# Top-k attention and a gated feed-forward on one core: stages of a unit set one unit apart

## The chip, the cores and the metric

One core of a Trainium2 chip runs the whole kernel in one launch. The metric is the time of an execution in microseconds (us). The engines named below are PE (TensorE), DVE (VectorE), ACT (ScalarE), POOL (GpSimd) and SP, which issues nearly all transfers. Each takes its instructions strictly in the order in which the program issued them.

## The reference

For 8 batches with 8 heads of 576 tokens and 64 dimensions, attention keeps of each row of scores only what is at least the 32nd largest; its output, 4608 tokens by 512, goes through `(h * cos(h)) @ w_out` with `h = x @ w_in`:

```python
scores = scale * np.matmul(q, k.transpose(0, 1, 3, 2))
kth = np.partition(scores, -top_k, axis=-1)[..., -top_k:-top_k + 1]
scores = np.where(scores >= kth, scores, -1000000000.0)
attn = np.exp(scores - np.max(scores, axis=-1, keepdims=True))
attn = attn / (np.sum(attn, axis=-1, keepdims=True) + 1e-09)
x = np.matmul(attn, v)      # then (B,H,S,D) -> (B*S, H*D)
h = x @ w_in
return (h * np.cos(h)) @ w_out
```

q, k and v are float32. The weights arrive as 64-bit floats and are decoded to float32 on the chip, in 32 chunks of 128x512.

## The kernel before

**Units and slots.** A unit is 128 tokens of one pair of heads: 36 token tiles by 4 pairs, 144 units. The main loop (L523) runs one slot per unit, and each engine's queue is filled in the order written there. For a unit, `scores` (L192, PE) writes a 4-bank PSUM tile, of which there is one; `take_scores` (L207, ACT) copies it to one of three score buffers `s`, a slot ahead of the ranking. `topk_round` (L214, DVE) runs four times: the 8 largest of each row, then (three times) their replacement by a very low value, for both heads. `bounds` (L230) makes from the first and the 32nd value the two bounds, with two small POOL operations; `mask` and `exponentials` (ACT, L241 and L249) apply them in place and sum the rows into `den`; `reciprocal` (DVE, L258) adds 1e-9 and inverts; `normalise` (POOL, L264) scales. `split` (L274) separates the 16-bit halves on POOL and writes them to DRAM by SP; `transposes` (L283) reads them back transposed by a DMA; `values` (L308, PE) multiplies by v, and `take_values` (ACT) puts the result in `xT`.

**Which slot does what.** In slot i: ranking of unit i and scores of unit i+1; bounds, mask, exponentials, reciprocal, normalising and split of unit i-1, the reciprocal standing in DVE's queue between the second and the third part of the ranking of unit i; transposes of unit i-2; values of unit i-3. The first eight units don't go through DRAM: PE transposes them in the slot of their normalising (`transposes_now`, L291).

**Feed-forward.** It is fed between attention's matmuls in jobs: `ff1` (L356; four 128x128 by 256 products, 8 matmul instructions, into one of two banks `mm`) and `ff2` (L437; two products of 512 columns, 4 instructions, into the single bank `o2`; eight jobs make a row of 128 tokens). `feed` (L478) alternates the two kinds as far as inputs are there, at most two and then four a slot within a credit of four a slot, capped at five. `take_banks` (L386), called at the head of the slot and behind the first feeding, empties full banks on ACT; only the second call of a slot comes behind the exponentials. POOL reduces the angles (`reduce_first`, `reduce_second`), ACT takes the sine (`sines`), POOL multiplies (`gate`). A block is 256 tokens, eight units (the first four and the last two are 128), and needs one tile `g` per 1024 values; a new one is begun only while live tiles and staged weight chunks are fewer than `CHUNKS` (L93).

**Weights.** `load_weights` stages a chunk, `decode_first` (ACT, three operations), `decode_second` (DVE, two, L132 and L133) and `decode_third` (POOL, two) decode it; DVE's part runs from slot 1 on, POOL's part behind the slot's split.

Of the kernel before, what the change touches and what calls it, by code (L numbers as in the profile page):

```python
# [10 lines left out]
F32 = mybir.dt.float32  # L11
# [3 lines left out]
AF = mybir.ActivationFunctionType  # L15
ALU = mybir.AluOpType

P = 128
TOPK = 32
NEG = -3.4028234663852886e38  # L20
EPS = 1e-9
# [10 lines left out]
def kernel(  # L32
# [9 lines left out]
    nc = tc.nc  # L42
# [22 lines left out]
    make_identity(nc, ident)  # L65
    halfpi = consts.tile([P, 1], F32, tag="halfpi")
    nc.vector.memset(halfpi, math.pi / 2.0)

# [18 lines left out]
    for f in range(NF):  # L89
        w = consts.tile([P, DM], F32, tag=f"w_out{f}", name=f"w_out{f}")  # L90
        w_out.append(w)
        chunks.append((moe_w_out[f * P : (f + 1) * P, :], w))
    CHUNKS, XB = 9, 4  # L93
    ff = {"live": 0, "tick": 0, "now": 0, "credit": 0.0, "end": False, "kind": 0}

    wq = {"next": 0, "loaded": deque(), "second": deque(), "done": 0, "ready": 0}

    def load_weights(n):
        for _ in range(n):
            i = wq["next"]  # L100
            if i >= len(chunks):
                return
            src, dst = chunks[i]
            if not DECODE:
                nc.sync.dma_start(out=dst, in_=src)
                wq["next"] = wq["done"] = i + 1
                continue
            staging = len(wq["loaded"]) + len(wq["second"])
            if staging >= 6 or staging + ff["live"] >= CHUNKS:
                return  # L110
            st = ffw.tile([P, CW, 2], I32, tag="g", name="st", bufs=CHUNKS)
            nc.sync.dma_start(out=st.rearrange("p w i -> p (w i)"), in_=src)
            wq["loaded"].append((st, dst))
            wq["next"] = i + 1
# [12 lines left out]
    def decode_second():  # L127


        for st, w in wq["second"]:  # L130
            wi = w.bitcast(I32)
            nc.vector.tensor_scalar(out=w, in0=w, scalar1=2.0, scalar2=None, op0=ALU.max)  # L132
            nc.vector.tensor_scalar(  # L133
                out=wi, in0=wi, scalar1=3, scalar2=None, op0=ALU.logical_shift_left
            )

    def decode_third():
        while wq["second"]:
            st, w = wq["second"].popleft()
            wi = w.bitcast(I32)  # L140
            nc.gpsimd.tensor_tensor(out=wi, in0=wi, in1=st[:, :, 0], op=ALU.add)
            nc.gpsimd.tensor_tensor(out=w, in0=w, in1=st[:, :, 1].bitcast(F32), op=ALU.mult)
            wq["done"] += 1
# [23 lines left out]

    def load_qk(b, hp):
        st = pairs.setdefault((b, hp), {})
        t = st["q"] = loads.tile([P, S], F32, tag="q", name="q")  # L170
        nc.sync.dma_start(out=t, in_=qT[b, 2 * hp : 2 * hp + 2].rearrange("h d s -> (h d) s"))

        t = st["k"] = loads.tile([P, S], F32, tag="k", name="k")
        nc.sync.dma_start(out=t[0:D], in_=kT[b, 2 * hp])
        nc.sync.dma_start(out=t[D:P, TAIL:S], in_=kT[b, 2 * hp + 1, :, 0:MAIN])
        nc.sync.dma_start(out=t[D:P, 0:TAIL], in_=kT[b, 2 * hp + 1, :, MAIN:S])

    def load_v(b, hp):
        st = pairs.setdefault((b, hp), {})
# [25 lines left out]
                    )  # L205

    def take_scores(u):  # L207
        s = u["s"] = work.tile([P, 2, S], F32, tag="s", name="s", bufs=3)
        nc.scalar.copy(  # L209
            out=s.rearrange("p j (h w) -> p (j h) w", h=2),  # L210
            in_=u.pop("sc").rearrange("p j h w -> p (j h) w")[:, :, 0:HS],
        )

    def topk_round(u, rnd):  # L214
        s = u["s"]
        if rnd == 0:
            u["m8"] = small.tile([P, 2, TOPK], F32, tag="m8", name="m8")
            u["rest"] = work.tile([P, 2, S], F32, tag="rest", name="rest", bufs=1)
        m8, rest = u["m8"], u["rest"]
        src = s if rnd == 0 else rest  # L220
        at = slice(8 * rnd, 8 * rnd + 8)
        for j in range(2):
            nc.vector.max(m8[:, j, at], src[:, j])  # L223
        if rnd < TOPK // 8 - 1:
            for j in range(2):
                nc.vector.match_replace(rest[:, j], m8[:, j, at], src[:, j], NEG)  # L226
        else:
            del u["rest"]

    def bounds(u):  # L230

        nb = small.tile([P, 2, 2], F32, tag="nb", name="nb")
        nc.gpsimd.tensor_scalar(  # L233
            out=nb, in0=u.pop("m8")[:, :, 0 : TOPK : TOPK - 1], scalar1=-SCALE,
            scalar2=1.0, op0=ALU.mult, op1=ALU.mult,
        )
        nd = small.tile([P, 2], F32, tag="nd", name="nd")
        nc.gpsimd.tensor_tensor(out=nd, in0=nb[:, :, 0], in1=nb[:, :, 1], op=ALU.subtract)
        u["nb"], u["nd"] = nb, nd

    def mask(u):  # L241

# [6 lines left out]
    def exponentials(u):  # L249
        s, nd = u["s"], u.pop("nd")  # L250
        den = u["den"] = small.tile([P, 2], F32, tag="den", name="den")
        for j in range(2):
# [2 lines left out]
                accum_out=den[:, j : j + 1],  # L255
            )

    def reciprocal(u):  # L258
        den = u.pop("den")
        nc.vector.tensor_scalar(out=den, in0=den, scalar1=EPS, scalar2=None, op0=ALU.add)  # L260
        u["rden"] = small.tile([P, 2], F32, tag="rden", name="rden")
        nc.vector.reciprocal(u["rden"], den)  # L262

    def normalise(u):  # L264
        s, rden = u["s"], u.pop("rden")
# [8 lines left out]
    def split(u):  # L274


        s = u.pop("s").rearrange("p j k -> p (j k)").bitcast(U16)
        halves = work.tile([P, 2, 2 * S], U16, tag="halves", name="halves", bufs=1)
        nc.gpsimd.tensor_copy(out=halves, in_=s.rearrange("p (k h) -> p h k", h=2))  # L279
        rows = u["rows"] = dram.tile([P, 2, 2 * S], U16, tag="rows", name="rows")  # L280
        nc.sync.dma_start(out=rows, in_=halves)

    def transposes(u):  # L283
        rows = u.pop("rows").rearrange("q h k -> (q h) k")
# [39 lines left out]
    def take_values(u):  # L324
        blk = block_of[u["tok"]]
        if "xT" not in blk:
            blk["xT"] = work.tile([P, NP, blk["w"]], F32, tag="xT", name="xT", bufs=4)
        at = u["tok"] - blk["t0"]
        nc.scalar.copy(out=blk["xT"][:, u["hp"], at : at + P], in_=u.pop("o")[:, 0:P])  # L329
        blk["left"] -= 1  # L330
# [55 lines left out]
    def take_banks():  # L386
        while full:
            take, *what = full.popleft()
            take(*what)
# [72 lines left out]
    def can_first():  # L462
        if not first:
            return False
        blk, i = first[0]
        if blk["left"] or wq["ready"] < (((i + 1) * (256 // blk["w"]) - 1) // FC + 1) * NC:
            return False
        staging = len(wq["loaded"]) + len(wq["second"])
        return i % 4 > 0 or ff["live"] + staging < CHUNKS

    def can_second():
        if not second:
# [27 lines left out]
            last[part[0], u["hp"]] = i  # L500
    at_slot = {}
    order = [(b, hp) for b in range(B) for hp in range(NP)]
    for load, bufs, behind in ((load_qk, 5, -1), (load_v, 5, 3)):
        for n in range(NP, len(order)):
            slot = last[order[n - bufs]] + behind if n >= bufs else NP + 2
            at_slot.setdefault(slot, []).append((load, *order[n]))
# [6 lines left out]


    EARLY = 2 * NP
    load_qk(0, 0)
    load_weights(1)
    load_qk(0, 1)
# [1 line left out]
    scores(units[0])  # L520
    take_scores(units[0])
    decode_first(3)
    for i in range(NU + 3):  # L523
        ff["end"] = i >= NU
        u, w, x, y = (units[i - n] if 0 <= i - n < NU else None for n in range(4))
        early = w and i - 1 < EARLY
        if x and i - 2 < EARLY:
            x = None
        if y and i - 3 < EARLY:
            y = None  # L530
        ff["credit"] = min(ff["credit"] + 4.0, 5.0)
        ff["now"] += 1
        wq["ready"] = wq["done"]
        if w:
            bounds(w)
        if u:
            if i > 0:
                decode_second()
            topk_round(u, 0)
        take_banks()  # L540
        if y:
            values(y)
        if i + 1 < NU:
            scores(units[i + 1])
        if y:
            take_values(y)
        if i + 1 < NU:
            take_scores(units[i + 1])
        for load, b, hp in at_slot.get(i, []):
            load(b, hp)  # L550
        if x:
            transposes(x)
        gate(1)
        if w:
            mask(w)
            exponentials(w)
        if early:
            reciprocal(w)
            normalise(w)
        if u:  # L560
            topk_round(u, 1)
        if w and not early:
            reciprocal(w)
            normalise(w)
            split(w)
        if u:
            topk_round(u, 2)
        feed(2)
        take_banks()
        if i > 0:  # L570
            decode_third()
            decode_first(3)
        load_weights(3)
        reduce_first()
        feed(4)
        if early:
            transposes_now(w)
            values(w)
            take_values(w)
        reduce_second()  # L580
        if u:
            topk_round(u, 3)
        sines(2)
    while first or second or full:
        ff["now"] += 1
        ff["credit"] = 2.0
# [44 lines left out]
```

## Time and profile before

| what | us |
|---|---|
| median of 3 runs | 1909.7 (1906.25 to 1910.59) |
| profiled execution, time | 1905.77 |
| profiled execution, span | 1904.0 |
| PE busy | 1524.3 |
| DVE busy | 1505.9 |
| POOL busy | 1161.5 |
| ACT busy | 987.7 |

The span runs from the first to the last instruction. Busy time counts what an engine executes; matmul ends are modelled, so PE's busy time includes matmuls that wait for each other. A group of rows further below carries the mark L and a line number of the kernel before. In a timeline, the bracket at the end of a row is the engine's idle time ahead of it and what ended that. In windows, PEclk is the granted clock as a share of full speed (1.0 is 2.4 GHz, 0.5 is 1.2 GHz).

### The profile page before, as it was taken

To read this page: it belongs to the slowest core of one execution; us is meant where nothing else is said; L and a number is where in the kernel's file an instruction comes from. 1 tells how busy PE (TensorE), PEld (TensorE's weight loads), DVE (VectorE), ACT (ScalarE), POOL (GpSimd) and SP (SyncE) were. 2 spreads that over 40 slices of the span, in tenths; PEclk is the share of its full clock that TensorE was granted. 3 is DMA by queue.
4 is the path that set the end of the run, shared out by engine and by line. 5 is a ranking of instruction groups with operands and counts; after the bars stand their busy time and mean duration, and the time that the engine had idled before them with its cause. 6 is when DMAs were issued, how large, how long until landed. Compare 5 with 4: busy or idle time off the path is not lost.

```text
span 1904.0 us, 24525 instructions
## 1 busy us (share of the span) xinstructions
PE 1524.3 (80%) x8392; PEld 984.6 (52%) x8392; DVE 1505.9 (79%) x3249; ACT 987.7 (52%) x1622; POOL 1161.5 (61%) x1124
## 2 busy tenths in 40 slices
PE   3647577777968888888888888888888898889898
PEld 2435355453636454545555555555555555555564
DVE  7989688887877888888888787878787887878721
ACT  6765454444455545554555455555555545555421
POOL 4677566366575757666666666666666666666610
PEclk9668789797989899999999898999999899999899
DMA  7323255334533345434543344434543354433320
GB/s 218 101 85 94 80 142 144 99 106 130 139 91 106 105 130 149 112 106 119 151 113 112 95 130 128 127 94 130 142 118 106 97 131 126 118 99 105 95 60 17
DMA packets 381501, 216.57 MB, mean 114 GB/s; under 512 B 330688, under 2 KB 347072, under 8 KB 381376
## 3 DMA queue, kind: packets, MB, share of 16 engines
q1 hardware_dynamic: 381376, 215.00, 40.2%
q8 instruction: 66, 1.08, 0.2%
q14 instruction: 59, 0.48, 0.1%
HBM read 45.09 MB, written 89.65 MB: 71 GB/s over the span
## 4 chain that ended last, share of the span: by engine, by line
PE 33%; POOL 32%; ACT 23%; issue 6%; DVE 3%; DMA 2%; SPq 0%; POOLq 0%; ACTq 0%; DVEq 0%
PE o L446 12%; PE mm L370 12%; POOL halves L279 8%; ACT s L253 7%; POOL x L417 7%; ACT s L245 5%; PE o L322 5%; PE sc L199 4%; POOL s L267 3%; ACT s L209 3%; POOL x L409 3%; POOL x L410 3%; POOL x L408 3%; POOL g L434 2%; ACT L253 2%
## 5 line engine op out<-in xcount | busy, mean ns | idle before, releaser
L446 PE MATMUL o<-w_out,g 128*128 128x512 f32 x1152 | 621.7, 677 | 235.3 <-ACT ob L455 143.2
L223 DVE MAX8 m<-rest 128x8 f32<-128x576 f32 x864 | 607.9, 745 | 0.0
L267 POOL TENSOR_SCALAR s<-s,rden 128x576 f32<-128x576 f32 x288 | 212.5, 749 | 573.0 <-DVE rden L262 291.1
L370 PE MATMUL mm<-xT,w_in 128*128 128x256 f32 (+1 forms) x2688 | 547.3, 356 | 4.3 <-ACT g L382 4.3
L370 PEld LDWEIGHTS mm<-xT,w_in 128*128 128x128 f32 x2688 | 462.1, 194 | 146.7 <-issue 96.3
L446 PEld LDWEIGHTS o<-w_out,g 128*128 128x128 f32 x1152 | 232.9, 215 | 514.0 <-issue 316.0
L226 DVE MATCH_REPLACE8 rest<-m,rest 128x576 f32<-128x576 f32 x576 | 423.4, 743 | 0.0
L245 ACT ACTIVATE s<-s,nb 128x576 f32<-128x576 f32 x288 | 207.4, 769 | 209.2 <-POOL nb L233 209.2
L279 POOL COPY halves<-s 128x2304 uint16<-128x2304 uint16 x136 | 286.8, 2109 | 8.6
L260 DVE TENSOR_SCALAR den<-den 128x2 f32<-128x2 f32 x144 | 24.1, 167 | 308.2 <-ACT s L253 307.8
L209 ACT COPY s<-sc 128x1152 f32<-128x1152 f32 x144 | 161.2, 1119 | 188.0 <-PE sc L199 107.6
L322 PE MATMUL o<-pT,v 128*64 128x128 f32 (+1 forms) x2560 | 174.2, 282 | 84.8 <-DMA pT<-rows 54.3
L253 ACT ACTIVATE s<-s,nd 128x576 f32<-128x576 f32 x288 | 219.4, 763 | 0.6
L322 PEld LDWEIGHTS o<-pT,v 128*64 128x64 f32 x2560 | 139.2, 145 | 152.4 <-issue 56.6
L226 DVE MATCH_REPLACE8 rest<-m,s 128x576 f32<-128x576 f32 x288 | 211.7, 743 | 0.0
L223 DVE MAX8 m<-s 128x8 f32<-128x576 f32 x288 | 202.1, 743 | 8.2 <-ACT s L209 8.2
L199 PE MATMUL sc<-k,q 64*128 64x288 f32 (+1 forms) x1280 | 196.5, 459 | 12.0 <-DMA k<-in_k_dram 8.5
L329 ACT COPY xT<-o 128x128 f32<-128x128 f32 x144 | 38.0, 264 | 302.6 <-PE o L322 302.4
L382 ACT ACTIVATE g<-mm 128x512 f32<-128x512 f32 x144 | 84.3, 586 | 164.9 <-PE mm L370 163.4
L417 POOL TENSOR_TENSOR x<-g,x 128x1024 f32<-128x1024 f32 x67 | 158.0, 2358 | 5.6
L434 POOL TENSOR_TENSOR g<-g,x 128x1024 f32<-128x1024 f32 x66 | 155.7, 2360 | 1.1 <-ACT x L427 0.9
L199 PEld LDWEIGHTS sc<-k,q 64*128 64x128 f32 (+1 forms) x1280 | 106.4, 191 | 58.1 <-issue 20.0
(45 smaller groups left out, 1019.7 us busy)
## 6 DMA issues: line engine op xcount, KB each, us to landing
rows<-halves SPq DMA_DIRECT2D x136, 576.0 KB, 2.8
q<-in_q_dram SPq DMA_DIRECT2D x32, 288.0 KB, 3.6
out_dram<-ob SPq DMA_DIRECT2D x36, 256.0 KB, 3.1
st<-in_moe_w_in_dram SPq DMA_DIRECT2D x16, 512.0 KB, 5.0
v<-in_v_dram SPq DMA_DIRECT2D x32, 256.0 KB, 3.8
st<-in_moe_w_out_dram SPq DMA_DIRECT2D x16, 512.0 KB, 3.3
k<-in_k_dram SPq DMA_DIRECT2D x32, 144.0 KB, 3.4
k<-in_k_dram SPq DMA_DIRECT2D x32, 128.0 KB, 3.8
```

Of the source, the lines that this page charges most:

```text
L199: nc.tensor.matmul(sc[r0 : r0 + rows, j, h, 0:HS], st["q"][d, q0 : q0 + rows], st["k"][d, h * HS : (h + 1) * HS], start=True, stop=True,)
L209: nc.scalar.copy(out=s.rearrange("p j (h w) -> p (j h) w", h=2), in_=u.pop("sc").rearrange("p j h w -> p (j h) w")[:, :, 0:HS],)
L223: nc.vector.max(m8[:, j, at], src[:, j])
L226: nc.vector.match_replace(rest[:, j], m8[:, j, at], src[:, j], NEG)
L245: nc.scalar.activation(out=s[:, j], in_=s[:, j], func=AF.Prelu, bias=nb[:, j, 1:2], scale=SCALE, alpha=FAR)
L253: nc.scalar.activation(out=s[:, j], in_=s[:, j], func=AF.Exp, bias=nd[:, j : j + 1], scale=1.0, accum_out=den[:, j : j + 1],)
L267: nc.gpsimd.tensor_scalar(out=s[:, j], in0=s[:, j], scalar1=rden[:, j : j + 1], scalar2=1.0, op0=ALU.mult, op1=ALU.mult,)
L279: nc.gpsimd.tensor_copy(out=halves, in_=s.rearrange("p (k h) -> p h k", h=2))
L322: nc.tensor.matmul(o[d, r], lhsT, rhs, start=c == 0, stop=c == NT)
L370: nc.tensor.matmul(mm[:, at : at + w], w_in[f // FC][:, c, (f % FC) * P : (f % FC + 1) * P], blk["xT"][:, c], start=c == 0, stop=c == NC - 1,)
L417: nc.gpsimd.tensor_tensor(out=x, in0=g, in1=x, op=ALU.subtract)
L446: nc.tensor.matmul(o, g[:, at : at + P], w_out[f], start=f == 0, stop=f == NF - 1)
```

## The change

From the ninth unit on, each stage has a slot of its own. In slot i: ranking of unit i, scores of i+1; bounds, mask and exponentials of i-1; reciprocal (now first in DVE's slot), normalising, split and write of i-2; transposes of i-3; values of i-4. The bounds are made by three small ACT operations in place of two of POOL, and ACT adds the 1e-9 that DVE added. There are four score buffers in place of three, and eight `g` tiles in place of nine. Loads of v stand one slot later. The first nine units have a loop body of their own: bounds, mask and exponentials of the unit before ahead of the copy of new scores, all four rankings in a row around the reciprocal, decoding on ACT and POOL in smaller pieces, three chunks a slot up to slot 5 and two after; DVE's decoding now begins in slot 0. For the very first pair, two of the three k transfers are issued by ACT's queue. Eight transposes of the identity run on PE at the start. The loop has one slot more. The body of the old loop is shown above; the rest of the diff is:

```diff
+    eps = consts.tile([P, 1], F32, tag="eps")
+    nc.vector.memset(eps, EPS)
...
-    CHUNKS, XB = 9, 4
+    CHUNKS, XB = 8, 4
...
-            staging = len(wq["loaded"]) + len(wq["second"])
-            if staging >= 6 or staging + ff["live"] >= CHUNKS:
+            if staged() + ff["live"] >= CHUNKS:
...
-        for st, w in wq["second"]:
+        while wq["second"]:
+            st, w = wq["second"].popleft()
...
+            wq["third"].append((st, w))
...
+    def decode_third(n):
+        for _ in range(min(n, len(wq["third"]))):
+            st, w = wq["third"].pop()
...
+        also = nc.sync if (b, hp) > (0, 0) else nc.scalar
...
-        nc.sync.dma_start(out=t[0:D], in_=kT[b, 2 * hp])
+        also.dma_start(out=t[0:D], in_=kT[b, 2 * hp])
         nc.sync.dma_start(out=t[D:P, TAIL:S], in_=kT[b, 2 * hp + 1, :, 0:MAIN])
-        nc.sync.dma_start(out=t[D:P, 0:TAIL], in_=kT[b, 2 * hp + 1, :, MAIN:S])
+        also.dma_start(out=t[D:P, 0:TAIL], in_=kT[b, 2 * hp + 1, :, MAIN:S])
...
-        s = u["s"] = work.tile([P, 2, S], F32, tag="s", name="s", bufs=3)
+        s = u["s"] = work.tile([P, 2, S], F32, tag="s", name="s", bufs=4)
...
+        m8 = u.pop("m8")
+        nb = u["nb"] = small.tile([P, 2, 2], F32, tag="nb", name="nb")
+        nc.scalar.mul(out=nb, in_=m8[:, :, 0 : TOPK : TOPK - 1], mul=-SCALE)
+        nd = u["nd"] = small.tile([P, 2], F32, tag="nd", name="nd")
+        for j in range(2):
+            nc.scalar.activation(
+                out=nd[:, j : j + 1], in_=m8[:, j, TOPK - 1 : TOPK], func=AF.Identity,
+                bias=nb[:, j, 0:1], scale=SCALE,
+            )
...
+        nc.scalar.activation(out=den, in_=den, func=AF.Identity, bias=eps, scale=1.0)
...
     def reciprocal(u):
-        den = u.pop("den")
-        nc.vector.tensor_scalar(out=den, in0=den, scalar1=EPS, scalar2=None, op0=ALU.add)
         u["rden"] = small.tile([P, 2], F32, tag="rden", name="rden")
-        nc.vector.reciprocal(u["rden"], den)
+        nc.vector.reciprocal(u["rden"], u.pop("den"))
...
-    for load, bufs, behind in ((load_qk, 5, -1), (load_v, 5, 3)):
+    for load, bufs, behind in ((load_qk, 5, -1), (load_v, 5, 4)):
...
+    def early_slot(i, u, w):
+        n = 3 if i < 6 else 2
+        decode_second()
+        topk_round(u, 0)
+        scores(units[i + 1])
+        for load, b, hp in at_slot.get(i, []):
+            load(b, hp)
+        load_weights(n)
+        if w:
+            bounds(w)
+            mask(w)
+            exponentials(w)
+            reciprocal(w)
+        topk_round(u, 1)
+        topk_round(u, 2)
+        topk_round(u, 3)
+        decode_third(1)
+        if w:
+            normalise(w)
+        take_banks()
+        take_scores(units[i + 1])
+        gate(1)
+        decode_third(2)
+        feed(2)
+        reduce_first()
+        reduce_second()
+        if i != NP:
+            decode_first(n - 1)
+        feed(2)
+        if w:
+            transposes_now(w)
+        decode_first(n - len(wq["second"]))
+        if w:
+            values(w)
+            take_values(w)
+        sines(2)
...
+    def slot(i, u, w, x, y, z):
+        decode_second()
+        if x:
+            reciprocal(x)
+        if u:
+            for rnd in range(TOPK // 8):
+                topk_round(u, rnd)
+        take_banks()
+        if z:
+            values(z)
+        if i + 1 < NU:
+            scores(units[i + 1])
+        if z:
+            take_values(z)
+        if i + 1 < NU:
+            take_scores(units[i + 1])
+        for load, b, hp in at_slot.get(i, []):
+            load(b, hp)
+        load_weights(2)
+        if y:
+            transposes(y)
+        gate(1)
+        if x:
+            normalise(x)
+            split(x)
+            write_halves(x)
+        if w:
+            bounds(w)
+            mask(w)
+            exponentials(w)
+        feed(2)
+        take_banks()
+        decode_third(2)
+        decode_first(2)
+        reduce_first()
+        reduce_second()
+        feed(4)
+        sines(2)
...
+    tt = ps.tile([P, 512], F32, tag="ot", name="warm", bufs=1)
+    for _ in range(8):
+        nc.tensor.transpose(tt[:, 0:P], ident, ident)
...
-    for i in range(NU + 3):
+    for i in range(NU + 4):
...
+        u, w = (units[i - n] if 0 <= i - n < NU else None for n in range(2))
+        x, y, z = (units[i - n] if EARLY <= i - n < NU else None for n in range(2, 5))
+        if i <= EARLY:
+            early_slot(i, u, w)
+        else:
+            slot(i, u, w, x, y, z)
```

## Rows read from the trace of the kernel before

**Rows 1.** The busy line of the page: engine, busy us, share, instructions

```profile
PE 1524.3 (80%) x8392; PEld 984.6 (52%) x8392; DVE 1505.9 (79%) x3249; ACT 987.7 (52%) x1622; POOL 1161.5 (61%) x1124
```

**Rows 2.** The page's chain that ended last, share of the span by engine

```profile
PE 33%; POOL 32%; ACT 23%; issue 6%; DVE 3%; DMA 2%; SPq 0%; POOLq 0%; ACTq 0%; DVEq 0%
```

**Rows 3.** The waits: who waited for whom, us in total, times, longest

```profile
DVE den L260 <- ACT s L253: 307.8, 111, 5.8
PE o L446 <- ACT ob L455: 143.2, 29, 5.9
PE o L446 <- POOL g L434: 81.2, 21, 11.3
```

**Rows 4.** The timeline of VectorE, one unit: start, us, engine, line

```profile
1055.28 1.41 DVE L223 MAX8 m<-s 128x8 f32<-128x576 f32 x2
...
1060.87 0.17 DVE L260 TENSOR_SCALAR den<-den 128x2 f32<-128x2 f32 x1
...
1065.25 1.40 DVE L223 MAX8 m<-s 128x8 f32<-128x576 f32 x2
```

**Rows 5.** Windows by stage: stretch and its length, busy us by engine, clock, DMA

```profile
9.04:213.95 204.91, 115.65 (x692) 85.68 (x692) 184.96 (x349) 130.40 (x232) 139.21 (x131) 0.76 0.38 113
213.95:472.53 258.58, 188.19 (x1187) 124.28 (x1188) 208.80 (x463) 126.93 (x209) 154.93 (x151) 0.84 0.44 121
472.53:1808.14 1335.61, 1130.86 (x6091) 718.88 (x6090) 1094.33 (x2421) 708.88 (x1152) 859.41 (x825) 0.92 0.42 117
1808.14:1904.00 95.86, 86.47 (x418) 54.02 (x416) 17.77 (x18) 19.09 (x28) 6.07 (x5) 0.99 0.13 39
1186.00:1188.90 2.90, 2.90 (x5) 1.24 (x4) 2.90 (x7) 0.00 (x0) 2.84 (x3) 0.52 0.03 6
```

**Rows 6.** The timeline of ScalarE, third stage, one unit and its neighbours

```profile
1184.47 0.57 ACT L455 ACTIVATE ob<-o 128x512 f32<-128x512 f32 x1
...
1192.02 0.27 ACT L329 COPY xT<-o 128x128 f32<-128x128 f32 x1 [0.75 <-PE o L322]
1193.21 1.12 ACT L209 COPY s<-sc 128x1152 f32<-128x1152 f32 x1 [0.93 <-PE sc L199]
1194.70 1.44 ACT L245 ACTIVATE s<-s,nb 128x576 f32<-128x576 f32 x2 [0.36 <-POOL nb L233]
1196.05 0.76 ACT L253 ACTIVATE s<-s,nd 128x576 f32<-128x576 f32 x1
...
1197.47 0.19 ACT L253 ACTIVATION_READ_ACCUMULATOR s<-s,nd 128x1 f32 x1
```

**Rows 7.** The timeline of TensorE, third stage

```profile
1065.52 1.09 PE L322 MATMUL o<-pT,v 128*64 128x128 f32 x16
...
1067.94 3.72 PE L370 MATMUL mm<-xT,w_in 128*128 128x256 f32 x16
...
1075.03 1.09 PE L322 MATMUL o<-pT,v 128*64 128x128 f32 x16
...
1177.34 1.89 PE L370 MATMUL mm<-xT,w_in 128*128 128x256 f32 x8
1185.10 3.78 PE L446 MATMUL o<-w_out,g 128*128 128x512 f32 x4 [5.87 <-ACT ob L455]
...
1222.85 1.98 PE L446 MATMUL o<-w_out,g 128*128 128x512 f32 x4
1230.10 6.91 PE L446 MATMUL o<-w_out,g 128*128 128x512 f32 x12 [5.27 <-ACT ob L455]
```

**Rows 8.** The timeline of VectorE and ScalarE at the start

```profile
9.04 1.42 DVE L223 MAX8 m<-s 128x8 f32<-128x576 f32 x2 [8.18 <-ACT s L209]
...
14.88 0.65 ACT L122 ACTIVATE w_in<-st 128x512 f32<-128x512 f32 x1
...
18.70 0.41 DVE L132 TENSOR_SCALAR w_in<-w_in 128x512 f32<-128x512 f32 x1
...
32.14 1.40 DVE L133 TENSOR_SCALAR w_in<-w_in 128x512 int32<-128x512 int32 x1
```

More of the change, by code (lines that the diff above doesn't have):

```diff
@@ L92, with staged @@
         chunks.append((moe_w_out[f * P : (f + 1) * P, :], w))
-    CHUNKS, XB = 9, 4
+    CHUNKS, XB = 8, 4
     ff = {"live": 0, "tick": 0, "now": 0, "credit": 0.0, "end": False, "kind": 0}
-    wq = {"next": 0, "loaded": deque(), "second": deque(), "done": 0, "ready": 0}
+    wq = {"next": 0, "loaded": deque(), "second": deque(), "third": deque(), "done": 0, "ready": 0}
+    def staged():
+        return sum(len(wq[k]) for k in ("loaded", "second", "third"))
     def load_weights(n):
@@ L135, in decode_second @@
             )
-    def decode_third():
-        while wq["second"]:
-            st, w = wq["second"].popleft()
+            wq["third"].append((st, w))
+    def decode_third(n):
+        for _ in range(min(n, len(wq["third"]))):
+            st, w = wq["third"].pop()
             wi = w.bitcast(I32)
@@ L230, in bounds @@
     def bounds(u):
[L232 to L239, printed above, removed]
+        m8 = u.pop("m8")
[7 more added lines that the diff above has]
+            )
     def mask(u):
@@ L279, in split, with write_halves @@
         nc.gpsimd.tensor_copy(out=halves, in_=s.rearrange("p (k h) -> p h k", h=2))
+        u["halves"] = halves
+    def write_halves(u):
         rows = u["rows"] = dram.tile([P, 2, 2 * S], U16, tag="rows", name="rows")
-        nc.sync.dma_start(out=rows, in_=halves)
+        nc.sync.dma_start(out=rows, in_=u.pop("halves"))
     def transposes(u):
@@ L467, in can_first @@
             return False
-        staging = len(wq["loaded"]) + len(wq["second"])
-        return i % 4 > 0 or ff["live"] + staging < CHUNKS
+        return i % 4 > 0 or ff["live"] + staged() < CHUNKS
     def can_second():
@@ L522 @@
     decode_first(3)
-    for i in range(NU + 3):
+    for i in range(NU + 4):
         ff["end"] = i >= NU
[L525 to L530, printed above, removed]
         ff["credit"] = min(ff["credit"] + 4.0, 5.0)
@@ L533 @@
         wq["ready"] = wq["done"]
[L534 to L583, printed above, removed]
+        u, w = (units[i - n] if 0 <= i - n < NU else None for n in range(2))
[4 more added lines that the diff above has]
+            slot(i, u, w, x, y, z)
     while first or second or full:
```

## The prediction

> **What bounds the kernel now.** I read the page's busy times first [rows 1]: VectorE and TensorE both show about 1,500 us of 1,904, so neither is full, and no engine alone explains the span. The chain of the end [rows 2] is spread over PE, POOL and ACT, with 3% on DVE: work is handed from engine to engine, and the hand-overs are the bound. The waits say which [rows 3]: DVE stands 307.8 us, in 111 of its 144 units, for the sum of the exponentials; TensorE stands 143.2 us for ScalarE to empty the one bank of the second product (29 times, about 4.9 us each) and 81.2 us for gated tiles.
>
> The four ranking rounds of a unit, unhindered, show the floor. From the first maxima of one unit (1055.28) to those of the next (1065.25) are 9.97 us, with the addition at 1060.87 directly behind the second round [rows 4]. The stages, cut at the first maxima of units 0, 13 and 34 and behind the last ranking [rows 5]: units 0 to 12 take 204.91 us, units 13 to 33 take 258.58 (12.3 each), units 34 to 143 take 1335.61 (12.14 each), and 95.86 us follow the last ranking. So about 2.2 us of each slot is waiting, and that is what the change is about.
>
> **Why DVE waits.** In a slot DVE runs two rounds of unit i and then wants the denominators of unit i-1. Between them lie, in series, POOL's two small operations, ScalarE's two masks and two exponentials. ScalarE reaches these only behind a copy of scores for which it waits on TensorE, and POOL's small operations queue behind whatever POOL still has.
>
> **The change, part by part.**
>
> *Stages one slot apart.* The reciprocal now takes a sum made a slot earlier. From its scores being copied, ScalarE needs 1.12 (copy) + three small operations + 1.35 (two masks, start to next start) + 1.6 (two exponentials with their sums) + one small operation [rows 6]. The small ones are not in the trace; the nearest rows are a sum read-out of 0.19 and a 128x128 copy of 0.27, so four cost 0.76 to 1.08 and I take 0.9, in the middle. The chain is 5.0 us, well under one ranking of 9.8. The DVE wait therefore goes, unless TensorE is late by more than the rest of a slot. DVE also loses the addition (0.17 and the gap behind it [rows 4]): 9.97 - 0.2 = 9.8 a slot. If the wait stays instead, a slot is what it is now.
>
> The Trainium skill, ScalarE: Activation LUTs, section Rules for kernel authors, budgets about 0.3 us for an activation whose bias is a pointer, and tells authors to keep additions and multiplications on VectorE. By its price the three small operations with a pointer bias and the one without come to about 1.1 us as an estimate, 0.2 more than I take, which would add some 0.4 us per eight slots and 6 us in all. Its advice speaks against the move; the rows here speak the other way, as DVE is the engine with 9.8 us of work in a slot.
>
> *ScalarE's load.* It is busy 708.88 us in the 110 units of the third stage [rows 5], 6.45 a slot; plus 0.9 makes 7.3, against 9.8. It does not bound, but it is served in order: what stands behind the exponentials waits for them.
>
> *POOL* loses two small operations of the 859.41 us it is busy there and stays near 7.4 a slot.
>
> *What is late next: TensorE.* One slot without stalls is 9.51 us from one unit's values (1065.52) to the next (1075.03), of which values and scores take 2.42 (the first product starts at 1067.94), so that each of the slot's four jobs takes 1.77 [rows 7]. Eight slots hold 32 feed-forward jobs (16 of each product) and eight times values and scores: 76 us. That is under DVE's 78.4, but not when the stalls at the second product's bank are added. The row of 128 tokens ends twice in eight slots, in the slot's first feeding; following the loop's counters, the places are the same after the change, one unit later. Once the next job is that product again (1222 to 1230: 5.27 us of stall), once a first product lies between (1177.34 to 1185.10: 5.87) [rows 7]. The bank is emptied by ScalarE behind the exponentials. When TensorE is the late one, the release comes 5.0 + 0.57 (the emptying [rows 6]) = 5.6 us after the scores; TensorE has one job of 1.77 in between in the one place and two in the other, so it stalls 3.8 and 2.1: 5.9 instead of 11.1. After such a stall it runs at 1.2 GHz, the lower of its two clocks, for a while: four matmuls in 3.78 us and twelve in 6.91 instead of 1.77 and 5.3, granted clock 0.52 in the first [rows 5, 7]; 3.6 us per eight slots now, and with shorter stalls I take 2.7. The stall for gated tiles (3.9 each) should go, since POOL comes to the gate without first waiting for the ranking. Sum: 76 + 5.9 + 2.7 = 84.6, 10.6 a slot. From both sides: 9.8 (DVE alone, TensorE ahead) and 76 + 11.1 + 3.6 = 90.7, 11.3 (stalls as now).
>
> *Units 13 to 33.* The blocks are narrow and the feed-forward jobs come in bursts with empty slots between, so that DVE's floor is nearer: 10.3 a slot, 216 us (206 to 258.6 as now).
>
> *The first slots.* DVE is busy 184.96 of 204.91 us [rows 5]. The decoding's second step now also runs in slot 0, ahead of the first ranking, and needs the first pass over three chunks. Now the ranking starts at 9.04, and the third chunk's pass at 14.88 [rows 8], held by its load. So the first maxima come near 14.88 + 0.65 + two steps of 0.43, 16.4, instead: 7 us lost. Two k pieces and the head's issues on another queue may give back about 1 us. On the other side, the two steps per chunk take 0.41 and about the same alone, but 1.40 beside POOL's third step [rows 8]; that step now runs early in the slot, beside the rankings, so that most shifts find POOL quiet. Thirteen rankings and 32 chunks at 0.85 are 13 x 9.8 + 27 = 155, on 16.4 a floor of 172 for the start of unit 13; as now plus 7 is 221. TensorE's cold clock (0.76 here), ScalarE's three decodes a slot and the first products in slots 5 and 6 keep it off the floor: 190 (213.95 now).
>
> The Trainium skill, SBUF — State Buffer, section Who interferes with whom, says that a VectorE operation in a two-port mode and a GpSimd one exclude each other for the whole instruction. The 0.41 and the 1.40 agree. By it, decodes beside POOL's reductions would still be blocked: with half of the 64 steps at 1.4 the floor of 172 would be 203, an estimate.
>
> *Eight chunks instead of nine, four score buffers.* By the counters no block of two live at once needs more than eight tiles, the products are fed in the same slots shifted by one, so nothing is lost in the steady stage. A fourth score buffer keeps unit i-2 while i+1 is copied. Transposes have a slot of their own, as before, with the write ahead of them in the slot before; SP's order (loads, weights, transpose, write) gains no wait for a later engine.
>
> *The end.* With one stage more, the counters leave 53 feed-forward jobs after the last ranking slot instead of 49, and four units' values instead of three: 4 x 1.77 + 1.3 = 8.4 on 95.86: 104.
>
> **The sum.** 190 + 216 + 110 x 10.6 (1166) + 104 = 1676, and 1.8 around the span (1905.77 to 1904.0): 1678. The profiled execution lies 3.9 below the median of the runs shown, so 1680.
>
> **Rivals.**
> 1. *DVE's floor is reached.* TensorE gets ahead in the bursts and its stalls use up its lead only. For it: 76 against 78.4 us per eight slots. Against it: the stalls end at ScalarE's pace and bring the lower clock. 190 + 131 x 9.8 + 104 + 2 = 1580. Chance 0.15.
> 2. *The stalls at the bank stay as they are.* TensorE ends them in step with ScalarE behind rankings as now, and keeps its present loss: 11.3 to 11.8 a slot, the latter with the gate's 3.9 per eight slots. With 11.0 in units 13 to 33 (230): 190 + 230 + 110 x 11.5 + 106 = 1791. For it: bank, order and in-order queue are untouched. Against it: part of today's 5 us is ScalarE's wait for POOL's small operations. Chance 0.24.
> 3. *Slower: TensorE waits in every slot.* With the small operations on ScalarE, the emptying of the first product's banks, too, comes behind the whole chain; if TensorE needed one in every slot, it would stall 5.6 - 3.5 = 2.1 and run cold for 2: 9.5 + 4.1 = 13.6 a slot, 190 + 131 x 13.6 + 106 = 2078. It decides against the change from a loss of 2.6 us in each slot (12.14 less 9.51). Against it: these banks are two and one is filled per slot. Chance 0.06.
> 4. *The wait only changes its place:* DVE's reciprocal, now the head of its slot, waits for sums as long as it did in the middle, and slots stay at 12.1; the early part and the end cancel. 1905. Against it: a 5 us chain has a whole slot. Chance 0.03.
>
> My forecast (10.2 to 11.0 a slot: 1630 to 1735) has 0.52.
>
> **How the numbers follow.** The range takes in the forecast, the upper part of rival 1 and rival 2 up to 11.5 a slot: 1600 to 1800; outside are rivals 3 and 4 (0.09), and about half of rival 1 and a little of rival 2 (0.1). What the measurement can tell from no change is about 0.2%. Faster: 0.52 + 0.15 + 0.24 = 0.91, with 0.01 of rival 4; same 0.02; slower 0.06.
>
> **What would show it.** Right: the DVE idle behind the sums falls from 308 us to under 60; starts of rankings 10 to 11 apart; TensorE's stall at the second product still there at two places per eight units, 2 to 4 us each; the first ranking starts near 16; about 104 us follow the last ranking. Wrong: DVE waits at the reciprocal in most slots (rival 4), the first product's matmuls wait for their emptying (rival 3), or bank stalls of over 5 us (rival 2).

## The result and the profile after

The changed kernel takes 1689.9 us (median of 4, 1687.5 to 1695.1) against 1908.0 in the same comparison: ratio 0.886, interval 0.8835 to 0.8885. The forecast was 1680, within 1600 to 1800.

The page's busy line, and its chain that ended last by engine, of the kernel after; they answer to [rows 1, 2]:

```profile
PE 1483.0 (88%) x8400; PEld 967.1 (57%) x8400; DVE 1457.4 (86%) x3107; ACT 1110.4 (66%) x2200; POOL 1100.0 (65%) x835
PE 67%; ACT 14%; DVE 6%; DMA 4%; POOL 4%; issue 3%; SPq 2%; ACTq 0%; POOLq 0%; DVEq 0%
```

The chain is now TensorE's, with ScalarE's hand-overs between: POOL has fallen from 32% to 4%. The waits of the kernel after (total us, times, longest), against [rows 3]:

```profile
DVE rden L270 <- ACT den L266: 131.8, 55, 6.9
PE o L457 <- ACT ob L466: 81.9, 30, 8.0
PE o L457 <- POOL g L445: 22.2, 7, 7.5
```

The windows of the kernel after, cut as [rows 5] were, and last one period of eight units (columns as there):

```profile
15.31:181.44 166.13, 105.36 (x664) 78.68 (x664) 159.25 (x332) 135.45 (x270) 128.84 (x106) 0.82 0.41 126
181.44:407.00 225.56, 180.91 (x1176) 121.10 (x1176) 205.11 (x444) 145.85 (x294) 144.41 (x107) 0.87 0.49 136
407.00:1583.11 1176.11, 1089.46 (x6043) 700.21 (x6044) 1071.16 (x2310) 799.82 (x1590) 812.19 (x601) 0.96 0.49 133
1583.11:1688.40 105.29, 99.20 (x495) 62.08 (x493) 19.30 (x20) 21.82 (x36) 12.67 (x9) 0.99 0.16 45
845.52:930.61 85.09, 79.45 (x418) 50.82 (x418) 77.82 (x170) 58.63 (x116) 59.66 (x44) 0.96 0.52 129
```

Unit 13 starts at 181.4 (forecast 190), units 13 to 33 take 225.6 (216), units 34 to 143 take 1176.1 or 10.69 each (1166, 10.6), the end 105.3 (104).

TensorE at the two stalls of such a period, with the twelve matmuls behind the longer one, then an undisturbed twelve (kernel after, timeline; the bracket is the idle time ahead):

```profile
828.38 8.10 PE L457 MATMUL o<-w_out,g 128*128 128x512 f32 x12 [3.73 <-ACT ob L466]
838.83 5.42 PE L457 MATMUL o<-w_out,g 128*128 128x512 f32 x12
872.97 1.98 PE L457 MATMUL o<-w_out,g 128*128 128x512 f32 x4 [1.91 <-ACT ob L466]
```

The clock granted over these three stretches (windows, columns as in [rows 5]; the clock is the last figure but two):

```profile
828.38:836.42 8.04, 8.04 (x13) 3.23 (x13) 8.04 (x18) 2.31 (x2) 7.81 (x7) 0.66 0.30 112
838.83:844.18 5.35, 5.35 (x15) 2.20 (x13) 0.67 (x2) 5.11 (x10) 0.00 (x0) 1.00 0.89 246
872.97:874.80 1.83, 1.83 (x5) 0.87 (x6) 1.83 (x5) 0.00 (x0) 1.75 (x2) 1.00 0.47 142
```

The stalls were forecast at 3.8 and 2.1, the loss at the lower clock at 2.7: it is 8.10 - 5.42 = 2.7, all behind the first. 76 + 3.73 + 1.91 + 2.7 = 84.3, measured 85.1.

### The profile page after: what moved, and what is told of

The parts are those of the page before. It is cut to its first block, busy times and chain, and to the rows that moved or that the text cites. A ratio compares the mean times of both kernels' runs of the same rounds, so it can differ in the third digit from the quotient of the medians.

```text
span 1688.4 us, 24574 instructions
## 1 busy us (share of the span) xinstructions
PE 1483.0 (88%) x8400; PEld 967.1 (57%) x8400; DVE 1457.4 (86%) x3107; ACT 1110.4 (66%) x2200; POOL 1100.0 (65%) x835
## 4 chain that ended last, share of the span: by engine, by line
PE 67%; ACT 14%; DVE 6%; DMA 4%; POOL 4%; issue 3%; SPq 2%; ACTq 0%; POOLq 0%; DVEq 0%
PE o L457 26%; PE mm L381 23%; PE o L333 10%; PE sc L206 8%; DMA pT<-rows 4%; ACT s L261 3%; ACT s L253 3%; DVE m L230 3%; ACT s L216 2%; DVE rest L233 2%; ACT ob L466 1%; ACT nd L244 1%; POOL g L445 1%; POOL halves L287 1%; POOL x L428 1%
## 5 line engine op out<-in xcount | busy, mean ns | idle before, releaser
L457 PE MATMUL o<-w_out,g 128*128 128x512 f32 x1152 | 592.3, 652 | 110.7 <-ACT ob L466 81.9
L457 PEld LDWEIGHTS o<-w_out,g 128*128 128x128 f32 x1152 | 224.8, 206 | 374.1 <-issue 250.7
L333 PE MATMUL o<-pT,v 128*64 128x128 f32 (+1 forms) x2560 | 170.0, 278 | 40.6 <-DMA pT<-rows 26.2
L206 PE MATMUL sc<-k,q 64*128 64x288 f32 (+1 forms) x1280 | 192.1, 447 | 7.7 <-DMA k<-in_k_dram 7.6
L333 PEld LDWEIGHTS o<-pT,v 128*64 128x64 f32 x2560 | 135.3, 143 | 108.2 <-issue 64.2
L270 DVE RECIPROCAL rden<-den 128x2 f32<-128x2 f32 x144 | 22.3, 155 | 131.8 <-ACT den L266 131.8
```

Of the source, the lines that this page charges most:

```text
L206: nc.tensor.matmul(sc[r0 : r0 + rows, j, h, 0:HS], st["q"][d, q0 : q0 + rows], st["k"][d, h * HS : (h + 1) * HS], start=True, stop=True,)
L333: nc.tensor.matmul(o[d, r], lhsT, rhs, start=c == 0, stop=c == NT)
L457: nc.tensor.matmul(o, g[:, at : at + P], w_out[f], start=f == 0, stop=f == NF - 1)
```

## The experiments

Medians of four or more executions, each beside the kernel before on the same chip (1908.5 to 1909.6).

**The bank first.** In the loop body of unit nine and later:

```diff
+        feed(2)
+        if any(f[0] is take_second for f in full):
+            take_banks()
         if w:
             bounds(w)
             mask(w)
             exponentials(w)
-        feed(2)
         take_banks()
```

> The changed kernel (1690 us), but in the slots in which a row of the second product ends, ScalarE empties that bank ahead of the bounds, mask and exponentials instead of behind them. Theory (TensorE with its stalls at this bank sets the slot): the stalls of 3.73 and 1.91 us per eight units shrink to under 1 and 0, the lower clock after the first goes, eight units fall from 85 us to near DVE's 8 x 9.75 = 78; over 110 units that is 95 us, so about 1590 (1570 to 1620). Rival (DVE's wait for the sums at the head of its slot is the bound, and the bank is hidden): the sums then come 1.3 us later in these two slots, so 1690 to 1735.

1584.5 us, ratio 0.8312 (0.8291 to 0.8333). Its third stage, TensorE's one remaining stall of that place (the bracket names the ScalarE operation behind the emptying) and DVE's wait for the sums (windows, timeline, waits):

```profile
400.94:1477.70 1076.76, 1051.82 (x6071) 689.55 (x6072) 1067.88 (x2311) 803.41 (x1592) 816.49 (x603) 1.00 0.53 146
791.79 5.39 PE L457 MATMUL o<-w_out,g 128*128 128x512 f32 x12 [0.78 <-ACT nb L241]
DVE rden L270 <- ACT den L266: 29.1, 23, 2.6
```

Units 66 to 83 now start 9.7 apart without exception; DVE is busy 1067.9 of the stage's 1076.8 us, and the granted clock is 1.00 (0.96 in the change). So the stalls at this bank, and the clock they cost, were what kept the changed kernel off DVE's floor. This is the version to keep of those tried here; it is 105 us better than the change.

**The stall filled.** In `ff2`, ahead of the new bank:

```diff
         if f0 == 0:
+            fill = ps.tile([P, 512], F32, tag="ot", name="fill", bufs=1)
+            for _ in range(14):
+                nc.tensor.transpose(fill[:, 0:P], ident, ident)
             blk["o"] = ps.tile([P, 512], F32, tag="o2", name="o2", bufs=1)
```

> The changed kernel, but ahead of each new row of the second product TensorE runs 14 transposes of the identity, about 1.8 us at full clock, whose result nobody reads, where it would stand still waiting for the bank. Theory (after the 3.7 us stall twelve matmuls take 8.1 us instead of 5.3 because the granted clock has fallen): half of the stall is filled, the clock stays up, 2.8 us per eight units less, 1690 - 38 = 1652 (1640 to 1690). Rival (the twelve are slow for another reason, such as their own inputs): no gain, 1690 to 1710.

1661.1 us, 29 less than the change. The longer stall in its timeline, and the window of the matmuls behind it:

```profile
813.53 1.69 PE L453 MATMUL fill<-ident 128*128 128x128 f32 x14
817.42 5.39 PE L460 MATMUL o<-w_out,g 128*128 128x512 f32 x12 [2.20 <-ACT ob L469]
817.42:822.74 5.32, 5.32 (x12) 2.18 (x12) 5.32 (x12) 2.31 (x2) 4.73 (x3) 1.00 0.17 65
```

The work is useless, and yet the same twelve matmuls take 5.39 us instead of 8.10, at a granted clock of 1.00 instead of 0.66: the slowness was the clock's, and about 29 of the 105 us of the bank are its share.

**More small operations.**

```diff
+        for _ in range(4):
+            more = small.tile([P, 2], F32, tag="more", name="more")
+            nc.scalar.activation(out=more, in_=den, func=AF.Identity, bias=eps, scale=1.0)
```

> The changed kernel with four more operations of 128x2 on ScalarE behind the addition to the sums, of no use, about 0.25 us each from start to start, 1.0 us per unit. Theory (the bank is released behind this chain, twice per eight units): each of the two stalls grows by 1.0, so 2 us per eight units plus some lower clock in the second, 1690 + 33 to 60: 1735 (1715 to 1755). Rival (ScalarE has room, 66% busy): 1690 to 1700.

1741.6 us, 52 more. The two stalls in its timeline:

```profile
853.73 8.05 PE L460 MATMUL o<-w_out,g 128*128 128x512 f32 x12 [4.61 <-ACT ob L469]
899.15 2.92 PE L460 MATMUL o<-w_out,g 128*128 128x512 f32 x4 [2.80 <-ACT ob L469]
```

Each has grown by 0.9 us, and behind the second four matmuls now take 2.92 instead of 1.98. ScalarE, 66% busy in the change, is on the path because TensorE's bank is released behind its chain.

**Stages back in one slot.** The reciprocal moves between the second and third round, all of `w`; loads of v, transposes and values one slot earlier:

```diff
-            reciprocal(x)
...
             exponentials(w)
+            reciprocal(w)
+            normalise(w)
+            split(w)
+            write_halves(w)
```

> The changed kernel, but from the ninth unit on reciprocal, normalising, split and write belong to the slot of the exponentials again, the reciprocal between the second and the third ranking round; transposes and values follow one slot earlier, v loads too. Small operations on ScalarE, four score buffers and the first nine units stay as changed. Theory (the separation of the stages gives the gain): most of it goes, DVE waits again in most slots, 1850 (1790 to 1910). Rival (the gain is from the bounds leaving POOL or from the fourth buffer): within 30 us of 1690.

1766.8 us, outside both ranges: 77 of the 218 us go, not 160. DVE waits 208.6 us for the sums, more than the change's 131.8 and less than the 307.8 of before: separation in time is one remedy among others.

**ScalarE's bounds alone, in the kernel before.** `bounds`, `exponentials` and `reciprocal` as in the change, `bounds` called ahead of `mask`; nothing else.

> The kernel before with the bounds made by ScalarE's three small operations, behind the copy of the scores, and the 1e-9 added there; nothing else. Theory: ScalarE no longer waits for POOL's small operations (209 us in all) but does 1.2 us more in each chain to the sums; the wait was partly POOL's reductions ahead of them, so a gain, 1830 (1780 to 1890). Rival (as in the changed kernel, where POOL's bounds were the faster ones): 1900 or more.

1798.8 us, ratio 0.9417 (0.9398 to 0.9436): half of the gain without any stage moved. What it takes away is ScalarE's wait for POOL's first small operation. That wait in the kernel before, then DVE's for the sums in this one (307.8 before):

```profile
ACT s L245 <- POOL nb L233: 209.2, 60, 13.1
DVE rden L265 <- ACT den L261: 231.0, 97, 8.1
```

**POOL's bounds in the changed kernel.**

```diff
         decode_second()
+        if w:
+            bounds(w)
         if x:
             reciprocal(x)
```

with `bounds`, the sum and the addition as in the kernel before.

> The changed kernel, but the bounds are made by POOL's two small operations at the head of its slot again and the 1e-9 is added by DVE; the stages stay a slot apart. Theory (what counts is the time from the scores to the release of the second product's bank): ScalarE's chain is 1.2 us shorter, but POOL comes to the bounds up to 2 us late in the slots behind its reductions; DVE's floor rises by 0.2 a slot. About even: 1700 (1670 to 1740). Rival (taking the bounds off POOL gave a good part of the gain): over 1760.

1649.0 us: 41 better than the change, and 21 beyond my range. Two things are moved at once here, the bounds to POOL and the addition to DVE. Rows of one execution, of 1666.7 us (the other three took 1648 to 1649): three waits, the addition (busy us in all, mean ns), and one meeting of POOL and DVE:

```profile
POOL nb L240 <- DVE den L268: 280.8, 90, 6.2
ACT s L252 <- POOL nb L240: 51.4, 28, 8.4
DVE den L268 <- ACT s L260: 15.1, 9, 3.8
L268 DVE TENSOR_SCALAR den<-den 128x2 f32<-128x2 f32 x144 | 82.0, 569 | 15.1 <-ACT s L260 15.1
852.76 2.36 POOL L428 TENSOR_TENSOR x<-g,x 128x1024 f32<-128x1024 f32 x1
852.80 2.34 DVE L268 TENSOR_SCALAR den<-den 128x2 f32<-128x2 f32 x1
```

The lateness of POOL that I feared hardly comes: in 90 slots POOL stands ahead of the bounds and waits for DVE, and ScalarE waits 51.4 us for the bounds where it waited 209.2 before. DVE's wait for the sums is nearly gone. But its addition, 0.15 us in most slots, takes over 1.6 in 25 slots of the third stage, 2.34 in the one shown, beside POOL's multiplication of 2.36; DVE is busy 82.0 us with additions, 24.1 in the kernel before. So the 41 us are a gain (POOL's bounds are in time, and ScalarE's chain is some 0.9 us shorter) less a loss by DVE's addition, and the two were not tried apart. With the stages separated, bounds and addition together cost more on ScalarE than off it.

**Both: the bank first, POOL's bounds,** the 1e-9 still on ScalarE:

> The kernel that empties the second product's bank ahead of the chain (1584 us), with the bounds on POOL, the 1e-9 still on ScalarE. Theory (once the bank no longer waits for the chain, the slot is DVE's 9.7, and the length of the chain costs nothing): 1584 within 8. Rival (the 41 us that POOL's bounds won in the changed kernel are ScalarE's load itself): 1545 to 1560.

1582.1 us (interval of the ratio 0.8266 to 0.8303, that of the bank first alone 0.8291 to 0.8333): no difference. With the bank out of its way, making the chain shorter by the bounds gains nothing; a longer chain was not tried there.

**Three score buffers in the changed kernel.**

```diff
-        s = u["s"] = work.tile([P, 2, S], F32, tag="s", name="s", bufs=4)
+        s = u["s"] = work.tile([P, 2, S], F32, tag="s", name="s", bufs=3)
```

> The changed kernel with three score buffers instead of four. Theory: the copy of the scores of unit i+1 must then wait for the split of unit i-2 in the same slot, which POOL ends 4 to 6 us into the slot; behind it stand bounds, mask and exponentials (5 us), so the slot becomes 11 to 12.5: 1690 + 110 x 1 = 1800 (1730 to 1900). Rival (the fourth buffer is not needed): 1690 to 1700.

1911.4 us: all of the gain goes, 111 us more than expected and beyond the range. One row of its waits:

```profile
ACT s L216 <- POOL halves L287: 430.0, 101, 9.2
```

The copy of scores waits for the split, the bounds stand behind the copy, and behind these DVE's sums (DVE waits 349.3 us for them) and TensorE's bank (222.5 us).

**Four score buffers, or eight tiles, in the kernel before.** `bufs=4` with `CHUNKS, XB = 8, 4`; and the latter alone:

> The kernel before with four score buffers (and eight tiles, for room), nothing else. Theory: ScalarE's copy waits 73.9 us in all for POOL's split of the unit three before; that goes, but DVE still waits for the sums: 1870 (1840 to 1912). Rival (the fourth buffer makes most of what is left of the gain when the stages are put back into one slot): under 1800.

> The kernel before with eight tiles for feed-forward blocks and weight chunks instead of nine. Theory (by the loop's counters two live blocks need no more than eight): no change, 1908 within 6 us. Rival (fewer tiles hold the feed-forward back): 1930 or more.

1915.2 and 1911.5 us against 1909.6 and 1908.7: the buffer alone brings nothing (0.3% the other way, where I expected 1870), and a tile less costs 0.2%. In the first, ScalarE's wait for the split goes, and its wait for POOL's bounds grows from 209.2 to 240.8.

**The start.** The body of the first nine units in the order of the kernel before, three chunks a slot:

> The changed kernel with the order of the first nine units as in the kernel before (bounds on ScalarE stay). Theory: unit 13 starts near 214 instead of 181, the rest is as in the changed kernel: 1690 + 33 = 1723 (1705 to 1735). Rival (what is gained at the start is given back in the next units, since the weights and the first products set these): 1690 to 1700.

1699.0 us: the new start is worth about 9 us, not 33; the interval of the ratio, 0.8873 to 0.8914, just overlaps the change's. The rival holds in part: unit 13 starts 16 us later than in the change (197.3 against 181.4), but units 13 to 33 then take 214.9 us instead of 225.6. That unit 13 starts at 197.3 and not at 214 is gained from unit 9 on, which starts as in the kernel before (150.2 against 150.6): there the slots are separated, and ScalarE's bounds alone, in the kernel before, start unit 13 at 208.2.

The next kernel leaves DVE's decoding out of slot 0. By the order in the code, POOL then finishes chunks out of their order, and some early products use weights not yet decoded, so it only shows what the time does:

```diff
-        decode_second()
+        if i > 0:
+            decode_second()
```

> The changed kernel, but DVE's part of the decoding does not run in slot 0, so the first ranking waits only for its scores. Theory: the first maxima start near 9 instead of 15.3, the three chunks are shifted in slot 1 instead (2.5 us), later slots of the start are held by ScalarE and TensorE too: 1690 - 4 (1682 to 1690). Rival (the start is bound by the weights, which now come later): 1690 to 1697.

1685.8 us: 4 below the change, with executions that overlap (1680.0 to 1689.3, the change's 1687.5 to 1695.1). The first maxima start at 10.68 instead of 15.31, but that gain can't be told from nothing in the time.

## Why the prediction was right, and where not

- *TensorE with its bank sets the slot:* right, shown from three sides (bank first 1584.5, stall filled 1661.1, chain lengthened 1741.6), and the sizes were right to 0.2 us a stall in the period shown.
- *DVE's wait falls under 60 us:* wrong, 131.8. It contradicted my own sum: at 10.6 a slot DVE must stand 0.8 in each, 88 us in units 34 to 143 alone. Nor do rankings start 10 to 11 apart: most start 9.7 apart, and DVE stands mostly in two slots of eight, about 6 us behind the longer stall and 1 to 1.6 behind the shorter, where TensorE is late by more than a slot can take up (timeline of the kernel after):

```profile
845.44 0.17 DVE L270 RECIPROCAL rden<-den 128x2 f32<-128x2 f32 x1 [5.94 <-ACT den L266]
895.13 0.17 DVE L270 RECIPROCAL rden<-den 128x2 f32<-128x2 f32 x1 [1.09 <-ACT den L266]
```

- *The separation removes the wait:* right as a mechanism (with POOL's bounds 15.1 us of the wait are left), too large as a cause. ScalarE's bounds alone give 110 of the 218 us, the change with POOL's bounds 260, with ScalarE's 218: both edits cut ScalarE's wait for POOL's bounds, 209.2 us before, and together they leave a longer chain ahead of the bank. I priced the small operations at 0.9 us, which their rows bear out, and charged them only with the stalls; having bounds and addition on ScalarE costs 41 us, with DVE's addition in the other scale.
- *ScalarE's price.* In the kernel after, the three operations take 0.63 from the start of the first to that of the mask (840.02 to 840.65), and the addition 0.29:

```profile
840.02 0.21 ACT L241 ACTIVATE nb<-m 128x4 f32<-128x4 f32 x1
840.26 0.48 ACT L244 ACTIVATE nd<-m,nb 128x1 f32<-128x1 f32 x2
840.65 1.42 ACT L253 ACTIVATE s<-s,nb 128x576 f32<-128x576 f32 x2
845.04 0.29 ACT L266 ACTIVATE den<-den,eps 128x2 f32<-128x2 f32 x1
```

The Trainium skill, ScalarE: Activation LUTs, section Rules for kernel authors, gives about 0.3 us for an activation with a pointer bias. The 0.29 agrees; in a row they overlap, two in 0.48 us.

- *Four buffers:* I called them what "keeps unit i-2 while i+1 is copied" and gave them no price. With three, the change is worth nothing (1911.4); the fourth, without the change, is worth nothing either (1915.2).
- *Eight tiles, the end (53 jobs), the units' places in the loop:* right; 105.3 against 104, and 0.2% for the tiles.
- *The start:* the first maxima came at 15.31 (16.4 forecast), and DVE's decoding steps lost most of their meetings with POOL: their mean fell from 0.72 to 0.42 us over the first half of the weights and from 1.10 to 0.75 over the second. The floor of 172 was nearer than I put it: 181.4.

  The Trainium skill, SBUF — State Buffer, section Who interferes with whom, says that a VectorE operation in a two-port mode and a GpSimd one exclude each other. The means agree; the start of 203 that I estimated with it did not come.
- *Units 13 to 33:* 225.6, not 216 (10.7 a slot, not 10.3). With the bank first they still take 220.0; what else holds them was not tried. That this miss of 9.6 and the start's of 8.6 the other way cancel in the sum is luck.
- *Rivals:* none decided. Rival 1's floor is what the bank first reaches; rival 2's stalls at today's size did not come.

What stays open: the price of POOL's bounds in the change with the addition left on ScalarE; the fourth buffer in the kernel before with ScalarE's bounds, where the copy waits 109.8 us for the split; and the eight transposes and the k transfers at the start, which were not tried alone.

## What to carry to other kernels

Look at what a release is queued behind: a single accumulation bank emptied by an in-order engine cost 105 us here, and emptying it ahead of a 5 us chain cost nothing that shows. Two edits that cure the same wait don't add up; try each alone, and each taken out of the whole. A stage moved by a slot needs its buffer: one buffer too few gave back all of 218 us.

## What the runs showed that I had not expected

Unread work paid, through TensorE's clock: 14 transposes in a stall kept the granted clock at 1.00 instead of 0.66 and twelve matmuls at 5.39 us instead of 8.10, and the kernel was 29 us faster. A stall of 1.91 us left the matmuls behind it at full pace (1.98 for four); one of 2.80, with the chain lengthened, did not (2.92 for four), nor did one of 3.73.

An addition of 128x2, 0.15 us on DVE, took 2.34 us beside a multiplication on POOL. In the change with POOL's bounds such additions took 82.0 us of DVE, the engine nearest to its limit.
